# Loading w_out's diagonal blocks straight into their zeroed tile, in a causal convolution and token-mixing kernel

## The chip, the cores and the metric

The kernel runs on one core of a Trainium2 chip. The metric is the device time of one execution in microseconds; the time before the change is the median of 5 runs, 154.5 us (154.42 to 154.63).

The core has five engines that run their own instruction streams and wait for each other through semaphores. In the profile PE is TensorE (matmuls) and PEld its weight loads, DVE is VectorE, ACT is ScalarE, POOL is GpSimd and SP is SyncE. All transfers share 16 DMA engines; here GpSimd issues the loads and SyncE the stores.

## The reference

```python
def _attn_ref(x, weight):                      # x: (8, 4224, 192), weight: (8, 7)
    w = softmax(weight, axis=-1)               # 7 taps for each of 8 heads of 24 channels
    x_pad = concat([zeros((B, 6, D)), x], axis=1)
    x_unf = x_pad[:, idx, :].reshape(B, S, K, H, group)
    return einsum('hk,bskhg->bshg', w, x_unf).reshape(B, S, D)

def _moe_ref(x, w_q, w_k, w_out):              # x is the result of the convolution
    wq, wk = x @ w_q, x @ w_k                  # (B, S, 64)
    W_tok = einsum('bsd,btd->bst', wq, wk) / 8
    mixed = einsum('bst,btd->bsd', W_tok, x)   # linear attention, no softmax
    return maximum(mixed, 0) @ w_out           # (B, S, 192)
```

There is no softmax in the second part, so the kernel never forms the 4224x4224 matrix. With y the convolved input, mixed = (y w_q) (w_k' y'y) / 8: a 192x192 Gram matrix of y, a small product M = w_k' (y'y) / 8 of 64x192, and then (y w_q) M.

## The kernel before, in words

**The work.** Each of the 8 batches has 4224 tokens, kept as two halves of 2112. A batch passes these steps, by the letters that the kernel uses:

- Loads of x from DRAM, float32 to bfloat16 on the way, issued by GpSimd (`load`, `rows`, line 338, and `last`, line 355, a short last chunk), into one of NX = 5 buffers XW. Batch 0 has 8 load groups, batch 1 four, the others two.
- Y: the convolution as matmuls with a band matrix (BAND) as weights, copied out of PSUM to Y in bfloat16.
- D: a duplicate of 64 columns of Y, so that Gram blocks can be read in one run. TD: a transpose on VectorE. G: Gram matmuls into PSUM bank 7, 6 for each of 18 chunks.
- Q: 48 small matmuls, y w_q, copied out to QT by two casts on VectorE and one on ScalarE. They fill four PSUM banks.
- GEV, MC: the Gram matrix is copied out, two blocks are transposed (ident, gs), six matmuls with WK give M (gs,wk and gt,wk), which is scaled into the tile M_SB in three pieces (line 1036 on VectorE, 1035 on ScalarE).
- Z: matmuls of QT with M_SB; ReLU on the way out of PSUM to ZT (1033 on ScalarE, 1034 on VectorE). For the last 64 tokens of each half, the remainder, the tile is ZR.
- O: matmuls of ZT with w_out, copied out to one of NO = 8 slots of the ring OUT (o_sb) and stored by SyncE (line 858).

**w_out on chip.** Its rows 0 to 127 are the tile WO1. Its rows 128 to 191 are needed for both halves of the sequence at once: ZT's third part has half 0 on partitions 0 to 63 and half 1 on 64 to 127. WO2 (128 x 384) is block diagonal: the 64x192 rows stand in partitions 0 to 63, columns 0 to 191, and again in partitions 64 to 127, columns 192 to 383, and the rest is zero. One matmul against WO2 gives both halves. WO2S (128 x 192) has the same rows twice, one above the other. It is used for the remainder, and in `fused`, where Z and O matmuls of 64 partitions run side by side.

WO2S is loaded with WO1 (`wload`, lines 517 to 519, semaphore group `wl[2]`). WO2 is zeroed by GpSimd (`z_wo2`, line 534), and a job of kind W copies the two blocks from WO2S into it (lines 888 to 891).

**The order.** The string ORDER, one letter for each job, sets the order in which a planner in the kernel places jobs, and with it TensorE's order. For each copy out of PSUM the planner takes ScalarE or VectorE, whichever its cost table lets finish first; a duplicate may also go to GpSimd. CLOCK holds the planner's due times: `wq`, `wk`, `wo` say when weights are taken to be there, `fetch` how long TensorE's code is taken to be on its way. PSUM banks 0 to 6 are handed out by when they come free; a matmul waits for the copy that empties its bank. GATES ties some stores to a load: the store of block n waits until a certain group of x has landed. Block n = 5 b + i is part i of batch b; the copy into a slot of OUT waits for the store of block n - 8. SyncE issues the stores in order.

**TensorE's code.** The class Ahead cuts TensorE's instructions by branches that are never taken, with a prefetch hint each, so that its code is asked for ahead of its use, in blocks of 256 instructions.

Of the kernel before, what the change touches and what calls it, by code (L numbers as in the profile page):

```python
# [16 lines left out]


ORDER = (
    "YYYDYDYDYGTDGGGGYDYYDGTGYYDTGDGGTYTWGGGGGHQGGGTEYYMYDYWMQZZDZZZYYGGZYTGGDGAOTGOT"  # L20
    "YGZZGDOHQGTGYGGYZODOZGYGZGYYGTGGEYYGDMYGGGMTTOGHGAZGYGYYOGTYGGZGZGZQOTGTGYGGYZOG"
    "EDZZYZhGOTGHTMGGDQTMOGZZOYZGZGTZOYTGGZYGGQZGTOQGTZOYYGDZZGZGTYYOGGOEYYGGMOZDHATO"
    "GYOMGZZTGYGGTZOQGZGDOTYGZOOGAZGYGZGZTTGYGQZGOGEAZOGTTGYGMYYGGGGMODhQGZHOGAGGTYYT"
    "GGZOTGQZYGDTGYYOGOGEZZYGDGAMGYTZGGATZOYOHGZGGGTYMQGOZYZGTGYZGATGTGYGZQOOGTAZOGEY"
    "DYGGGYGGGTMAMYOOZZZGGGZDQOTZGOGAOGZTGTGAGGGQGZEOZOMZOZMOZOTZZZOOZOZOQZOZZZOOZZZO"
    "ZOOOOOO"
)


CLOCK = {  # L30
    "x0": (5.0, 7.5, 8.9, 8.1, 10.0, 11.8, 12.8, 13.6), "band": 6.5, "wq": 14.0, "wk": 16.0,
    "wo": 22.5, "fill": 24.0,
    "dma": (377e3, 13.2, 1.6, {"x": 2.2, "o": 1.2}), 
    "fetch": (64, 256, ((26.0, 8.5), (98.0, 6.4), (121.0, 7.3), (999.0, 4.8))),
}


# [192 lines left out]
def bass_lightweight_conv__then__hypermixer_token_mlp_kernel(  # L230
# [8 lines left out]
    B, S, D = x.shape  # L239
# [6 lines left out]
    wq_t, wk_t, wo_t = moe_w_q.tensor, moe_w_k.tensor, moe_w_out.tensor  # L246
# [16 lines left out]
    P = Program(nc, es)  # L263
# [50 lines left out]
    ]] + [[((0, 1), 0, 9, PAIRS), ((0, 1), 9, 18, PAIRS)]] * (B - 2)  # L314
    xg = [[P.group(f"x{b}_{g}") for g in range(len(GROUPS[b]))] for b in range(B)]
    wg = P.group("wg")
    wl = [P.group(f"wl{i}") for i in range(3)]
    og = [P.group(f"o{i}") for i in range(NO)]

    def dve(fn, deps=()):  # L320
# [2 lines left out]
    def act(fn, deps=()):  # L323
        return P.op("act", fn, deps)

    def pool(fn, deps=(), us=0.42):
        spent[0] += us
        return P.op("pool", fn, [*deps, *[o for o in P.ops["pool"] if o.dma is None][-1:]])
# [74 lines left out]
    rows(0, 1, 14, 0, 128, 3, xg[0][7], ())  # L403


    def wload(o, src, row0, width, grp, twice=1):
        spent[0] += 0.67
        n = o.shape[0]
        dims = [[width, n], [0, 2], [1, width]] if twice == 2 else [[width, n], [1, width]]
        P.dma("pool", lambda e: e.dma_start(o, bass.AP(src, row0 * width, dims)), grp)  # L410

    def warm(n, deps):
        def f(e):
# [18 lines left out]
    for j in range(5):  # L432
# [5 lines left out]
        if j == 0:  # L438
            eye = dve(lambda e: e.tensor_scalar(W_EYE[:, :], BITS[0:H, :], 127, None,
                                                op0=ALU.is_equal), [bits])  # L440
    zero = {1: [act(lambda e: e.memzero(XW[:, 1, :, NCK - 1, :]))]}
    fine = [XW[:, 0, g, 1 - g : 6 - g, :].rearrange("p c d -> p (c d)") for g in range(2)]
    x_cast = act(lambda e: e.copy(fine[0], staged[0]), [xg[0][0]])
    d = dve(lambda e: e.reciprocal(W_SM[:, :], W_SM[:, :]), [a])
# [35 lines left out]
    band = []  # L480
# [34 lines left out]
    load(1, 0)  # L515
    load(1, 1)
    wload(WO1[:, :], wo_t, 0, D, wl[2])
    wload(WO2S[0:64, :], wo_t, 128, D, wl[2])
    wload(WO2S[64:128, :], wo_t, 128, D, wl[2])
    wq = [pool(lambda e: e.tensor_copy(WQ[:, :, :], WSQ[:, :, :]), [wl[0]], 0.55)]  # L520
    z_wk = pool(lambda e: e.memset(WK[:, 3:6], 0.0))
    load(1, 2)
# [8 lines left out]
    )  # L531
    load(1, 3)
    load(2, 0)
    z_wo2 = pool(lambda e: e.memset(WO2[:, :], 0.0))
    load(2, 1)
    z_zr = pool(lambda e: e.memset(ZR[:, :, 1, :], 0.0), (), 0.34)
    for b in range(3, NX):
        load(b, 0)
# [12 lines left out]

    for o in wq:
        o.end = CLOCK["wq"]
    made = {"wq": wq, "wk": [z_wk], "wo": [z_wo2], "band": band, "ident": [ident], "z_m": [z_m], "z_zr": [z_zr]}
    done = {}

    def job_y1(b, g, k):
# [247 lines left out]
    def job_o(b, i, q):  # L805
        n = 5 * b + i
        orr = n % NO
        rem = i == 4
        tail = b == B - 1 and i == 3

        def pe(e, bk):
            kw = dict(skip_group_check=True)
            z = ZR[:, b % 2] if rem else ZT[:, (4 * b + i) % NZ]
            if rem:
                o = PS[:, bk, 0:192]
                e.matmul(o, z[:, 0, 0:128], WO1[:, :], start=True, stop=False, **kw)
                return e.matmul(o, z[:, 1, 0:128], WO2S[:, :], start=False, stop=True, **kw)
            for j in range(1 if tail else 2):
                cols = slice(q if tail else 2 * q + j, 512, 4)
                o = PS[:, bk + j, :]  # L820
                for h in range(2):
                    e.matmul(o[:, 192 * h : 192 * h + 192], z[:, h, cols], WO1[:, :],
                             start=h == 0, stop=False, **kw)
                last = e.matmul(o[:, 0:384], z[:, 2, cols], WO2[:, :], start=False, stop=True, **kw)
            return last

        def make(bk, swap=False):
            if swap:
                return [(OUT[:, orr, :, 384 * q : 384 * q + 384], PS[:, bk : bk + 2, 0:384])]
            if rem:  # L830
                return [(OUT[:, orr, 0, 0:192], PS[:, bk, 0:192])]
            if tail:
                return [(OUT[:, orr, q // 2, 384 * (q % 2) : 384 * (q % 2) + 384], PS[:, bk, 0:384])]
            return [(
                OUT[:, orr, :, 384 * q : 384 * q + 384].rearrange("p h (r d) -> p r h d", r=2),
                PS[:, bk : bk + 2, 0:384].rearrange("p r (h d) -> p r h d", h=2),
            )]

        def then():
            if not rem and q == 0 and not tail:  # L840
                return
            evs = [o for k in range(0 if not tail else q, q + 1) for o in made[("OUT", b, i, k)]]
            gate = GATES.get(n, -1)
            wait = [xg[1 + gate // 4 if gate < 4 else gate // 2][gate % (4 if gate < 4 else 2)]] * (gate >= 0)
            at = (b * S + 512 * i) * D
            if rem:
                parts = [(at + h * HALF * D, [[D, 64], [1, D]], OUT[64 * h : 64 * h + 64, orr, 0, 0:D])
                         for h in range(2)]
            elif tail:
                parts = [(at + q * D, [[4 * D, 128], [HALF * D, 2], [1, D]],  # L850
                          OUT[:, orr, q // 2, 384 * (q % 2) : 384 * (q % 2) + 384]
                          .rearrange("p (h d) -> p h d", h=2))]
            else:
                parts = [(at, [[4 * D, 128], [HALF * D, 2], [1, 4 * D]], OUT[:, orr, :, :])]
            for at, dims, src in parts:
                st = P.dma(
                    "sp",
                    lambda e, at=at, dims=dims, src=src: e.dma_start(bass.AP(out_t, at, dims), src),
                    og[orr], evs + wait,
                )  # L860
            made[("ST", n)] = [st]
            st.end = max(o.end for o in evs) + 3.0

            def landed(t, st=st):
                st.end = t

            queue["o"].append((max(o.end for o in evs) + DELAY,
                               (64 * 2 * D if rem else 128 * 2 * D if tail else 128 * 8 * D) * 4,
                               landed, GATES.get(n, -1)))
            flow()  # L870

        return Job(
            ("O", b, i, q), 1 if rem or tail else 2,
            pe, [192, 192] if rem else [192, 192, 384] * (1 if tail else 2),
            reads=[("WO", k) for k in range(2)] + [("Z", b, i, k) for k in range(1 if rem else 3)],
            evacs=[(make, ("OUT", b, i, q), 192 if rem else 384 if tail else 768, "copy")],
            then=then,
        )
# [5 lines left out]
            evacs=[(lambda bk, o=o, i=i: [(o, i)], ("WK", k), 128, "copy") for k, (o, i) in enumerate((  # L884
                (WK[0:64, 3], WK[0:64, 0]), (WK[64:128, 4], WK[64:128, 0]),
                (WK[64:128, 5], WK[64:128, 1]),
            ))]),
        Job(("W", "o", 1), 0, None, [], reads=["wo"], groups=[wl[2]],
            evacs=[(lambda bk, o=o, i=i: [(o, i)], ("WO", k), 192, "copy") for k, (o, i) in enumerate((
                (WO2[0:64, 0:D], WO2S[0:64, :]), (WO2[64:128, D : 2 * D], WO2S[64:128, :]),  # L890
            ))]),
    ]

# [75 lines left out]

    for (b, part), t in sent.items():  # L970
        put(b, part, t)
    for k, name in ((1, "wk"), (2, "wo")):
        x_at[id(wl[k])] = CLOCK[name]
    for o in band:
        o.end = CLOCK["band"]
# [180 lines left out]
    def fused(n):  # L1156
# [22 lines left out]
        def tails(e):  # L1179
            for h in range(2):  # L1180
                rows = slice(64 * h, 64 * h + 64)
                e.matmul(
                    PS[:, za[h], :], M_SB[rows, b % 2, 256 * h : 256 * h + 128],
                    QT[rows, b % 2, 512 * i : 512 * i + 512], start=True, stop=True, **kw,
                )
            for bk, z, cols in parts:
                for r in range(2):
                    for h in range(2):
                        rows = slice(64 * h, 64 * h + 64)
                        last = e.matmul(PS[:, bk + h, 192 * r : 192 * r + 192], z[rows, 2, cols[r]],  # L1190
                                        WO2S[rows, :], start=r == 0, stop=False, **kw)
            return last

        def heads(e):
# [74 lines left out]
```

## Time and profile before

| | us |
|---|---|
| median of 5 runs | 154.5 |
| lowest, highest | 154.42, 154.63 |
| profiled execution, its own time | 154.44 |
| span of its instructions | 152.6 |
| busy: PE | 137.3 (90%) |
| busy: ACT | 128.4 (84%) |
| busy: DVE | 119.5 (78%) |
| busy: POOL | 59.5 (39%) |

The TensorE clock granted in the profiled execution was 0.99 of full speed. 40.84 MB were moved, 268 GB/s over the span. The 16 DMA engines are busy for nine tenths or more of nearly every slice of the span up to 115 us. The loads (queue q0) took 73.9% of the engines' time, the stores and the few loads of SyncE (q1) 48.9%; the shares overlap. The packets of TensorE's code are a queue of their own, 19 packets of 0.31 MB in all.

How to read the rows that follow: a row of the chain gives start, length and what ran; a row of a timeline gives start, length, engine, line, operation, output<-input with shapes, and in brackets how long the engine stood idle before it and what ended that. A row of DMA issues ends with size and microseconds from issue to landing. Line numbers are those of the kernel before.

### The profile page before, as it was taken

How to read it: one execution, taken by the hardware profiler on the slowest of the kernel's cores; microseconds unless marked ns; L12 is line 12 of the kernel's file. 1: busy time of each engine (PE TensorE's matmuls, PEld its weight loads, DVE VectorE, ACT ScalarE, POOL GpSimd, SP SyncE). 2: the span in 40 equal slices, each digit the busy share in tenths (PEclk: the TensorE clock that was granted, in tenths of full speed). 3: DMA queues.
4: the chain of work that ended last, by engine and by line, in shares of the span. 5: the costliest groups of instructions: out<-in, count | busy, mean ns of one | idle time of the engine just before them, and what ended most of it. 6: DMA issues, size and time to landing. Idle time of an engine off the chain costs nothing.

```text
span 152.6 us, 5675 instructions
## 1 busy us (share of the span) xinstructions
PE 137.3 (90%) x2432; PEld 100.9 (66%) x2457; DVE 119.5 (78%) x241; ACT 128.4 (84%) x212; POOL 59.5 (39%) x77
## 2 busy tenths in 40 slices
PE   5977787999999999999999999999899999999920
PEld 1366565777767777677776777678577778766710
DVE  5674889966997877888988859999998977795710
ACT  5556598999998899988999989899898888999930
POOL 7999999989755801635200022030110300000000
PEclk9999999999999999999999999999999999999996
DMA  3999999999999999999999999999999978499896
GB/s 95 260 202 181 190 190 176 194 189 194 190 193 193 222 345 335 282 191 293 340 340 212 196 343 338 306 187 314 410 391 404 385 278 337 172 391 379 304 359 202
DMA packets 48984, 40.84 MB, mean 268 GB/s; under 512 B 37312, under 2 KB 41024, under 8 KB 48960
## 3 DMA queue, kind: packets, MB, share of 16 engines
q0 software_dynamic: 36384, 13.35, 73.9%
q1 hardware_dynamic: 12576, 27.14, 48.9%
q8 instruction: 19, 0.31, 0.7%
q14 instruction: 5, 0.04, 0.1%
HBM read 27.86 MB, written 25.95 MB: 353 GB/s over the span
## 4 chain that ended last, share of the span: by engine, by line
PE 74%; POOL 13%; DVE 5%; issue 3%; ACT 0%; ACTq 0%; POOLq 0%
PE ps L207 74%; POOL xw L338 7%; POOL wk L410 1%; DVE m_sb L1036 1%; DVE zt L1034 1%; POOL xw L355 1%; DVE zr L1034 1%; POOL wo2s L410 1%; DVE wo L1030 1%; DVE yb L1026 1%; DVE o_sb L1030 1%; DVE qt L1030 1%; POOL m_sb L523 1%; POOL wo L410 0%; POOL wq L520 0%
## 5 line engine op out<-in xcount | busy, mean ns | idle before, releaser
L1030 ACT COPY o_sb<-ps 128x768 f32<-128x768 f32 (+2 forms) x62 | 47.0, 772 | 3.5 <-PE ps L207 2.3
L207 PE MATMUL ps<-wo,zt 128*128 128x192 bf16 (+1 forms) x358 | 47.6, 271 | 0.8 <-DVE o_sb L1030 0.2
L1030 ACT CAST y<-ps 128x864 bf16<-128x864 f32 (+6 forms) x50 | 40.5, 838 | 5.4 <-PE ps L207 4.9
L207 PEld LDWEIGHTS ps<-y 128*128 128x128 bf16 (+1 forms) x864 | 35.5, 98 | 12.3 <-issue 2.4
L207 PE MATMUL ps<-y 128*128 128x64 bf16 (+1 forms) x864 | 40.2, 193 | 1.7 <-DVE yb L1026 0.6
L207 PEld LDWEIGHTS ps<-wo,zt 128*128 128x128 bf16 x358 | 31.9, 115 | 9.1 <-DVE o_sb L1030 0.6
L1030 POOL COPY y<-y 128x1152 bf16<-128x1152 bf16 x12 | 13.8, 1148 | 57.5 <-ACT y L1030 34.5
L1026 DVE STREAM_TRANSPOSE yb<-y 128x576 int32<-128x576 int32 x48 | 35.7, 759 | 0.1
L1034 DVE TENSOR_SCALAR zt<-ps 128x512 bf16<-128x512 f32 x46 | 30.7, 681 | 5.5 <-PE ps L207 5.2
L207 PE MATMUL ps<-xw,band 128*128 128x432 bf16 (+5 forms) x192 | 32.1, 286 | 2.6 <-DMA xw<-in_x_dram 1.2
L338 POOL DMA_DIRECT2D xw<-in_x_dram x35 | 32.1, 927 | 2.0 <-POOL xw L497 1.1
L1033 ACT ACTIVATE zt<-ps 128x512 bf16<-128x512 f32 x50 | 29.2, 604 | 1.7 <-PE ps L207 1.6
L207 PE MATMUL ps<-qt,m_sb 128*128 128x512 bf16 (+2 forms) x95 | 22.0, 334 | 1.4 <-DVE m_sb L1036 1.0
L1030 DVE CAST y<-ps 128x864 bf16<-128x864 f32 (+2 forms) x18 | 18.4, 1024 | 4.6 <-PE ps L207 4.1
L207 PEld LDWEIGHTS ps<-xw,band 128*128 128x128 bf16 x192 | 13.3, 97 | 8.3 <-DMA xw<-in_x_dram 1.6
L1030 DVE CAST qt<-ps 128x288 bf16<-128x288 f32 (+1 forms) x32 | 12.2, 424 | 7.7 <-PE ps L207 7.6
L207 PE MATMUL ps<-yb,wq 32*64 32x288 bf16 x768 | 15.3, 284 | 0.6 <-DVE y L1030 0.3
L1030 ACT CAST qt<-ps 128x576 bf16<-128x576 f32 x16 | 10.3, 643 | 4.3 <-PE ps L207 3.6
L207 PEld LDWEIGHTS ps<-qt,m_sb 128*128 128x128 bf16 (+1 forms) x120 | 8.9, 96 | 5.4 <-DVE m_sb L1036 1.1
L207 PEld LDWEIGHTS ps<-yb,wq 32*64 32x64 bf16 x768 | 10.6, 102 | 2.6 <-issue 0.7
L1030 DVE COPY o_sb<-ps 128x192 f32<-128x192 f32 (+2 forms) x12 | 7.4, 613 | 1.3 <-PE ps L207 1.0
L207 PE MATMUL ps<-warm 128*128 128x256 bf16 (+1 forms) x22 | 6.8, 434 | 1.3 <-DVE warm L389 1.3
(65 smaller groups left out, 73.1 us busy)
## 6 DMA issues: line engine op xcount, KB each, us to landing
out_dram<-o_sb SPq DMA_DIRECT2D x31, 768.0 KB, 7.4
xw<-in_x_dram POOLq DMA_DIRECT2D x14, 432.0 KB, 15.8
xw<-in_x_dram POOLq DMA_DIRECT2D x14, 384.0 KB, 16.9
o_sb<-in_x_dram SPq DMA_DIRECT2D x2, 480.0 KB, 4.7
out_dram<-o_sb SPq DMA_DIRECT2D x16, 48.0 KB, 6.0
out_dram<-o_sb SPq DMA_DIRECT2D x4, 192.0 KB, 2.4
xw<-in_x_dram POOLq DMA_DIRECT2D x2, 240.0 KB, 6.5
xw<-in_x_dram POOLq DMA_DIRECT2D x1, 288.0 KB, 6.9
```

The lines of the kernel that those rows point to most:

```text
L207: return self.e.matmul(*a, **k)
L338: return e.dma_start(XW[lo:hi, b % NX, half, c : c + n, :], bass.AP(x_t, at, [[D, hi - lo], [CW * D, n], [1, D]]),)
L355: lambda e: e.dma_start(XW[0:hi, b % NX, :, NCK - 1, :], bass.AP(x_t, at, [[D, hi], [HALF * D, 2], [1, D]]),),
L410: P.dma("pool", lambda e: e.dma_start(o, bass.AP(src, row0 * width, dims)), grp)
L523: z_m = pool(lambda e: e.memset(M_SB[:, :, :], 0.0), (), 0.85)
L1026: return e.transpose(o, i)
L1030: return e.copy(o, i) if eng == "act" else e.tensor_copy(o, i)
L1033: return e.activation(o, i, AF.Relu)
L1034: return e.tensor_scalar(o, i, 0.0, None, op0=ALU.max)
L1036: else e.tensor_scalar(o, i, scale, None, op0=ALU.mult))
```

## The change

WO2 is zeroed on ScalarE, early, instead of on GpSimd. The two blocks of w_out are loaded straight into WO2, in the place where WO2S was loaded, and these loads wait for the zeroing. The W job with the two copies is gone, and so is its letter in ORDER. WO2S is loaded by two later DMAs, behind the loads of batch 2, under a semaphore group of its own, `wl[3]`, for which the remainder's O matmuls wait. `fused` reads its 64-partition operands from the blocks of WO2. O jobs wait for the group `wl[2]` itself. Three due times in CLOCK are changed. With the new due times the planner also gives a few copies to other engines: near 20 to 27 us two casts of Y go from ScalarE to VectorE, one piece of M_SB and one ReLU from VectorE to ScalarE, and one duplicate of batch 2 goes from GpSimd to VectorE. Apart from that the order on each engine stays as it was.

```diff
-    "YYYDYDYDYGTDGGGGYDYYDGTGYYDTGDGGTYTWGGGGGHQGGGTEYYMYDYWMQZZDZZZYYGGZYTGGDGAOTGOT"
+    "YYYDYDYDYGTDGGGGYDYYDGTGYYDTGDGGTYTWGGGGGHQGGGTEYYMYDYMQZZDZZZYYGGZYTGGDGAOTGOTY"
...
-    "wo": 22.5, "fill": 24.0,
+    "wo": 21.0, "wo2": 36.0, "fill": 24.0,
...
-    "fetch": (64, 256, ((26.0, 8.5), (98.0, 6.4), (121.0, 7.3), (999.0, 4.8))),
+    "fetch": (64, 256, ((26.0, 6.6), (98.0, 6.1), (121.0, 6.5), (999.0, 4.8))),
...
-    wl = [P.group(f"wl{i}") for i in range(3)]
+    wl = [P.group(f"wl{i}") for i in range(4)]
...
-    def wload(o, src, row0, width, grp, twice=1):
+    def wload(o, src, row0, width, grp, twice=1, deps=()):
...
+    z_wo2 = act(lambda e: e.memzero(WO2[:, :]))
     fine = [XW[:, 0, g, 1 - g : 6 - g, :].rearrange("p c d -> p (c d)") for g in range(2)]
...
     wload(WO1[:, :], wo_t, 0, D, wl[2])
-    wload(WO2S[0:64, :], wo_t, 128, D, wl[2])
-    wload(WO2S[64:128, :], wo_t, 128, D, wl[2])
+    wload(WO2[0:64, 0:D], wo_t, 128, D, wl[2], 1, [z_wo2])
+    wload(WO2[64:128, D : 2 * D], wo_t, 128, D, wl[2], 1, [z_wo2])
...
     load(2, 0)
-    z_wo2 = pool(lambda e: e.memset(WO2[:, :], 0.0))
     load(2, 1)
+    for h in range(2):
+        wload(WO2S[64 * h : 64 * h + 64, :], wo_t, 128, D, wl[3])
...
-            reads=[("WO", k) for k in range(2)] + [("Z", b, i, k) for k in range(1 if rem else 3)],
+            reads=[("Z", b, i, k) for k in range(1 if rem else 3)],
+            groups=[wl[2], wl[3]] if rem else [wl[2]],
...
-        Job(("W", "o", 1), 0, None, [], reads=["wo"], groups=[wl[2]],
-            evacs=[(lambda bk, o=o, i=i: [(o, i)], ("WO", k), 192, "copy") for k, (o, i) in enumerate((
-                (WO2[0:64, 0:D], WO2S[0:64, :]), (WO2[64:128, D : 2 * D], WO2S[64:128, :]),
-            ))]),
...
-                                        WO2S[rows, :], start=r == 0, stop=False, **kw)
+                                        WO2[rows, D * h : D * h + D], start=r == 0, stop=False, **kw)
```

More of the change, by code (lines that the diff above doesn't have):

```diff
@@ L19 @@
 ORDER = (
-    "YYYDYDYDYGTDGGGGYDYYDGTGYYDTGDGGTYTWGGGGGHQGGGTEYYMYDYWMQZZDZZZYYGGZYTGGDGAOTGOT"
[L21 to L26, printed above, removed]
+    "YYYDYDYDYGTDGGGGYDYYDGTGYYDTGDGGTYTWGGGGGHQGGGTEYYMYDYMQZZDZZZYYGGZYTGGDGAOTGOTY"
+    "GZZGDOHQGTGYGGYZODOZGYGZGYYGTGGEYYGDMYGGGMTTOGHGAZGYGYYOGTYGGZGZGZQOTGTGYGGYZOGE"
+    "DZZYZhGOTGHTMGGDQTMOGZZOYZGZGTZOYTGGZYGGQZGTOQGTZOYYGDZZGZGTYYOGGOEYYGGMOZDHATOG"
+    "YOMGZZTGYGGTZOQGZGDOTYGZOOGAZGYGZGZTTGYGQZGOGEAZOGTTGYGMYYGGGGMODhQGZHOGAGGTYYTG"
+    "GZOTGQZYGDTGYYOGOGEZZYGDGAMGYTZGGATZOYOHGZGGGTYMQGOZYZGTGYZGATGTGYGZQOOGTAZOGEYD"
+    "YGGGYGGGTMAMYOOZZZGGGZDQOTZGOGAOGZTGTGAGGGQGZEOZOMZOZMOZOTZZZOOZOZOQZOZZZOOZZZOZ"
+    "OOOOOO"
 )
@@ L409, in wload @@
         dims = [[width, n], [0, 2], [1, width]] if twice == 2 else [[width, n], [1, width]]
-        P.dma("pool", lambda e: e.dma_start(o, bass.AP(src, row0 * width, dims)), grp)
+        P.dma("pool", lambda e: e.dma_start(o, bass.AP(src, row0 * width, dims)), grp, deps)
     def warm(n, deps):
@@ L553, in bass_lightweight_conv__then__hypermixer_token_mlp_kernel @@
         o.end = CLOCK["wq"]
-    made = {"wq": wq, "wk": [z_wk], "wo": [z_wo2], "band": band, "ident": [ident], "z_m": [z_m], "z_zr": [z_zr]}
+    made = {"wq": wq, "wk": [z_wk], "band": band, "ident": [ident], "z_m": [z_m], "z_zr": [z_zr]}
     done = {}
@@ L971, in bass_lightweight_conv__then__hypermixer_token_mlp_kernel @@
         put(b, part, t)
-    for k, name in ((1, "wk"), (2, "wo")):
+    for k, name in ((1, "wk"), (2, "wo"), (3, "wo2")):
         x_at[id(wl[k])] = CLOCK[name]
```

## The prediction

> **What bounds the kernel now.** I read the chain of work that ended last first, then the timelines of the engines around the change, then the transfers, because this kernel fills TensorE, ScalarE and the DMA queues at once. The chain, in order of time, columns start, length, what:
>
> ```profile
> 19.64 1.99 POOL xw L338 x2
> 21.63 0.48 POOL wo L534
> 22.11 0.02 issue
> 22.14 0.80 DVE wo L1030
> 22.93 0.03 issue
> 22.96 0.21 DVE wo L1030
> 23.17 0.03 issue
> 23.21 0.36 DVE m_sb L1036
> 23.57 0.27 issue
> 23.84 3.36 PE ps L207 x47
> ```
>
> Up to 23.8 us the end is set by GpSimd issuing loads; the last links are the memset of WO2 (L534), the two copies into it, and the scaling into M_SB that stands behind them on VectorE. From 23.84 us on the chain is TensorE almost alone. So what the stage before 24 us gives back can reach the end, unless something later was only just in time. The timeline of TensorE and VectorE there (start, length, engine, line, what, idle before):
>
> ```profile
> 21.23 0.25 PE L207 MATMUL ps<-gt,wk 128*128 128x64 bf16 x3
> 21.81 1.01 PE L207 MATMUL ps<-yb,wq 32*64 32x288 bf16 x48 [0.32 <-DVE y L1030]
> 22.14 1.04 DVE L1030 COPY wo<-wo2s 64x192 bf16<-64x192 bf16 x2 [0.35 <-POOL wo L534]
> 22.47 0.38 ACT L1035 ACTIVATE m_sb<-ps 64x128 bf16<-64x128 f32 x2
> 22.88 0.64 ACT L1030 CAST qt<-ps 128x576 bf16<-128x576 f32 x1
> 23.48 0.75 DVE L1030 CAST qt<-ps 128x288 bf16<-128x288 f32 x2
> 23.84 1.05 PE L207 MATMUL ps<-qt,m_sb 128*128 128x512 bf16 x4 [1.02 <-DVE m_sb L1036]
> 24.04 1.58 ACT L1033 ACTIVATE zt<-ps 128x512 bf16<-128x512 f32 x3 [0.52 <-PE ps L207]
> 24.28 0.11 PEld L207 LDWEIGHTS ps<-qt,m_sb 128*128 128x128 bf16 x2 [0.34 <-DVE qt L1030]
> ```
>
> TensorE stands 1.02 us for M_SB, and the fourth of its Z matmuls waits for the VectorE casts of QT, which stand behind the same copies. In the busy rows by stage TensorE then has 54.77 us of 55.70 (24 to 79.7 us) and 50.25 of 51.80 (89.2 to 141 us). What else could be late next is a transfer. The timeline of ScalarE at 79 us, and the store that was issued at 67.13 us (size, us to landing):
>
> ```profile
> 79.27 0.60 ACT L1033 ACTIVATE zt<-ps 128x512 bf16<-128x512 f32 x1
> 79.77 0.79 ACT L1030 COPY o_sb<-ps 128x768 f32<-128x768 f32 x1
> 80.48 0.88 ACT L1030 CAST y<-ps 128x864 bf16<-128x864 f32 x1
> ```
>
> ```profile
> out_dram<-o_sb SPq DMA_DIRECT2D x1, 768.0 KB, 12.3
> ```
>
> The OUT ring has 8 slots. The copy at 79.77 us is the first into slot 7 for block 15 (batch 3, i = 0) and must wait for the store of block 7, landed at 67.13 + 12.3 = 79.44 us. Its slack is 0.33 us, the smallest of all 32 reuses (the next are 1.37, 1.41 and 1.78 us, for blocks 20, 18 and 14).
>
> **The change, part by part.** Times are of the profiled run: 154.44 us, span 152.6, so 1.84 us lie around the span; the median of the runs is 154.5, 0.06 above.
>
> 1. *The copies leave VectorE.* Gone are 0.35 us of waiting for L534 and 1.04 us of copies. The built order also moves work: VectorE takes two of ScalarE's casts of Y (864 elements: 1.06 us on VectorE, 0.89 on ScalarE), ScalarE takes the 64x192 scaling (0.32; it was 0.35 on VectorE) and one 128x512 relu (0.60; 0.69). ScalarE gets 1.78 - 0.92 = 0.86 us lighter by 28 us, VectorE 2.12 - 1.04 - 0.35 - 0.69 = 0.04 heavier. New times: ScalarE's first Y cast of the pair at 20.76 ends near 21.6, the three M_SB pieces (0.32 + 0.38) by 22.3; their matmuls ended at 21.48. So M_SB is no longer last: the Q matmuls end at 22.82, and Z can start at 22.9 instead of 23.84, 0.93 earlier. What is late next are the evacuations. VectorE ends its duplicate at 21.79, then the new Y cast at 22.85, then the QT casts by 23.6 instead of 24.23: 0.6 earlier for the fourth Z. ScalarE ends its QT cast at 23.52 and starts the first relu there instead of at 24.04: 0.5 earlier. I take a lead of 0.60; bounds 0.5 and 0.93. A loss is excluded in this stage, since neither engine gets 0.1 us more work than before.
> 2. *Zeroing WO2 on ScalarE.* One more memset like L441 (0.345 us) between L441, which starts at 2.6 us, and the cast L443, before which ScalarE idles 2.0 us for a DMA: 0. The GpSimd loads of WO2 wait for it at 12.7 us, nine microseconds after it is done: 0, also for the WQ cast and batch 1's loads queued behind them.
> 3. *GpSimd's queue.* The memset (0.48) goes, two issues of WO2S (1.18, the row of L410 at 12.67) come behind batch 2. The loads of batches 3 and 4 are issued 0.70 later. Their time to landing rises from 6.4 us for a load issued at 18 us to 13.3 us at 28 us, so they wait in the DMA queue, not for the issue: 0. Were the queue empty: 0.70 on these loads, of which TensorE sees nothing, as batch 3's first part landed at 39.74 and was first read at 42.38, 2.6 us of slack.
> 4. *New waits of TensorE.* For the w_out loads at 27.2 us (landed by 20.2) and for WO2S at the first remainder, 43.7 us. WO2S lands right behind batch 2 (its last load: 23.79 + 10.2 = 34.0), at about 34.3, nine microseconds early. Both 0.
> 5. *A duplicate of batch 2 moves from GpSimd (1.16 us at 35.36) to VectorE.* The 576-element copies there took 0.28 to 0.61, so twice that is 0.6 to 1.2 us; it goes ahead of a relu before which VectorE idled 0.83. I take 0, at most 0.4, and that on an engine which has 16.55 us busy of 20.
> 6. *More bytes in the load queue.* 128 rows of 768 bytes. Batch 1's third part landed at 15.71 + 6.7 = 22.4, its fourth, 1,024 rows, at 18.00 + 6.4 = 24.4: 2.0 ns a row, so 0.26 us. Upper bound: the three w_out loads before the third part. The second part landed at 19.5, so w_out and the 1,112 rows of the third part took 2.9 us together, 0.7 of it w_out. Lower bound 0. Every later load, and the stores that are gated on loads, shift by 0.26: block 7's store lands at 79.70.
>
>    The Trainium skill speaks against this step: its page "DMA: Bandwidth & Descriptors", section Bandwidth (Measured), says that transfers under 64 KB are descriptor-dominated and gives 0.68 us for 4 KB and 0.95 for 64 KB. By an estimate from that page two 24 KB loads would cost about 1.6 us of queue, block 15 would be 1.3 us later than now, and the sum would end near 155. The rows above price three such loads at 0.7, so I go by them.
> 7. *The lead meets the ring.* With a lead of 0.60 ScalarE wants slot 7 at 79.17; it may have it at about 79.75. Its lead is gone there (79.77 before). TensorE keeps more: the Q matmuls at 81.87 need the banks that the cast at 80.48 empties, at 81.36, so TensorE can hold 81.87 - 81.42 = 0.45. ScalarE gains again where it had idled for TensorE: 0.21 at 82.89, then 0.18 at 88.55 and 0.33 at 89.21. By 90 us both have some 0.4. Bounds: 0.02 (ScalarE's lead at the ring sets all) and 0.60 (nothing lost). I take 0.40, as the idle rows exist.
> 8. *To the end.* The other ring slacks (1.37 and more, less 0.26) exceed the lead. The last full stores are issued when their copies end (141.15 for a copy that ended at 141.12), so the lead carries over one to one.
>
> Sum: 154.44 - 0.60 + 0.20 = 154.04; on the median 154.1.
>
> **The rivals.**
> A. *The ring takes nothing*: the lead stays 0.6 to 0.9, 153.6 to 153.9. For it: TensorE runs ahead by several banks, and ScalarE is 0.86 us lighter. Against: ScalarE waits in order, 0.33 us is less than 0.60.
> B. *The ring takes all*: 154.4 to 154.5. For it: ScalarE is busy 8.79 of 9.5 us after the ring. Against: the three idle rows.
> C. *Slower: TensorE's code comes late.* Its code is fetched in blocks through the same DMA engines. From a prefetch hint to the end of the block's packet took 5.0 to 10.1 us; counted in instructions, with blocks of 256 as the class Ahead has them and the hinted one 380 after its hint, the blocks hinted at 50.85 and 57.57 us came only 0.28 and 0.25 us before TensorE reached them, 8.65 and 8.62 us after the hint. With TensorE 0.6 us earlier against the loads and stores, another latency is drawn. It decides if one of these two exceeds 8.9; at 10.1 TensorE stands 1.2 us. Less the lead that is 0.6 of loss, and no more to lose at the ring: 155.0. Against: before, none of the hints stalled TensorE.
> D. *Slower through the ring*: two loads dearer than 1.0 us shift slot 7 past what TensorE can hold. Against: 0.7 is the upper bound by rows; 154.8 at 1.1.
>
> **How the numbers follow.** About 0.2%, 0.31 us, is what a measurement of this kernel can tell from no change: faster means below 154.19. Forecast (154.0 to 154.3) 0.40, A 0.27, B 0.15, C 0.13, D 0.05. Four fifths of the forecast's share, with A, are faster: 0.59, taken as 0.60; B and the rest of the forecast are the same: 0.23, taken as 0.22; C and D slower: 0.18. The likeliest case gives 154.1. The range reaches down through most of A, 153.6, and up to part of C and D, 154.8. The forecast's own range is 153.95 to 154.35.
>
> **What would show it.** Step 1: the Z matmuls start near 22.9 us, no wait of TensorE for M_SB, the fourth Z by 23.7. Step 6: the loads of batch 3 land 0.2 to 0.4 later, block 7's store at 79.6 to 79.9. Step 7: ScalarE's copy of block 15 shows idle time before it, released by a DMA; TensorE's lead is 0.6 before 79 us and about 0.4 after 90. Rival A shows no such idle time. C shows TensorE idle for "issue" over 0.3 us after a branch hint. The prediction is wrong if the lead at 28 us isn't near 0.6, or if the copy of block 15 doesn't wait.

## The result, and the profile after

The changed kernel takes 154.14 us in the median of 25 executions, the kernel before 154.54 in the median of the 46 beside it: a ratio of 0.9965, interval 0.9952 to 0.9978. The ratios, here and below, are of means, from which two slow executions of experiments are left out (157.09 and 156.67 us) while a few of the kernel before near 156 us are kept, so they lie up to 0.2% below the ratios of the medians, which is 0.9974 here. By the medians the change gains 0.40 us, a quarter of a per cent; 154.1 was forecast. But the executions do not sit at their median. Ten of the 25 took 153.65 to 153.86 us, eight 153.95 to 154.34, six 154.37 to 154.51 and one 155.03. The profiled execution is one of the early ones: 153.70 us, span 151.9.

Its chain of waits around the change (start, length, what; line numbers differ from those of the kernel before by one or two, and again in the experiments):

```profile
20.18 1.58 DVE y L1029 x2
21.77 0.02 issue
21.79 1.02 PE ps L207 x47
22.81 0.02 issue
22.83 0.78 DVE qt L1029 x2
23.61 0.14 issue
23.74 2.27 PE ps L207 x27
```

GpSimd, the memset and the two copies are gone from it. What is left is Y, the Q matmuls, VectorE's two casts of QT, and Z. The timeline there:

```profile
21.51 0.74 ACT L1034 ACTIVATE m_sb<-ps 64x192 bf16<-64x192 f32 x3
21.68 1.03 DVE L1029 CAST y<-ps 128x864 bf16<-128x864 f32 x1
21.79 0.99 PE L207 MATMUL ps<-yb,wq 32*64 32x288 bf16 x48 [0.32 <-DVE y L1029]
22.70 0.33 PEld L207 LDWEIGHTS ps<-qt,m_sb 128*128 128x128 bf16 x3 [0.23 <-issue]
22.93 0.59 PE L207 MATMUL ps<-qt,m_sb 128*128 128x512 bf16 x2 [0.16 <-DVE y L1029]
23.37 1.58 ACT L1032 ACTIVATE zt<-ps 128x512 bf16<-128x512 f32 x3
23.71 0.13 PEld L207 LDWEIGHTS ps<-qt,m_sb 128*128 128x128 bf16 x2 [0.68 <-ACT qt L1029]
23.74 0.59 PE L207 MATMUL ps<-qt,m_sb 128*128 128x512 bf16 x2 [0.22 <-DVE qt L1029]
```

The weight loads of Z in the profile of before:

```profile
23.61 0.33 PEld L207 LDWEIGHTS ps<-qt,m_sb 128*128 128x128 bf16 x3 [1.09 <-DVE m_sb L1036]
```

M_SB is now complete at 22.25 (21.51 + 0.74), before the Q matmuls end at 22.78. Both profiles have five weight loads of Z and only four matmuls: the record of the first matmul is missing. By the weight loads Z starts at 22.70 instead of 23.61, and its fourth matmul is loaded at 23.71 instead of 24.28 (the row is in the prediction). The 0.16 us before 22.93 is the missing record and no wait: in three later executions of the same program the first Z matmul is recorded at 22.69 to 22.72, with no idle time before it. For the same reason the wait for M_SB before was nearer 0.8 us (22.82 to 23.61) than 1.02. What is left is 0.22 us for the casts of QT. Now ScalarE at the ring, and the store of block 7 (size, us to landing):

```profile
78.47 0.60 ACT L1032 ACTIVATE zt<-ps 128x512 bf16<-128x512 f32 x1
78.96 0.79 ACT L1029 COPY o_sb<-ps 128x768 f32<-128x768 f32 x1
79.67 0.88 ACT L1029 CAST y<-ps 128x864 bf16<-128x864 f32 x1
```

```profile
out_dram<-o_sb SPq DMA_DIRECT2D x1, 768.0 KB, 11.5
```

Block 15's copy starts 0.81 us earlier than before and waits for nothing, because the store, issued at 66.86, landed at 78.40, a microsecond earlier than in the profile of before. In this execution hardly any of the lead was lost: ScalarE's copies near the end lie 0.76 us ahead (140.94 for 141.70), and the time is 0.74 lower.

Called lead below is how much earlier TensorE starts the first Y matmul of a load group than in the kernel before, where it starts at 24.73 (batch 1, third part), 57.64 (batch 4) and 92.38 us (batch 6). Here it is 0.56, 0.80 and 0.80.

### The profile page after: what moved, and what is told of

It reads as the page before. It is cut to its first block, busy times and chain, and to the rows that moved or that the text cites. A ratio compares the mean times of both kernels' runs of the same rounds, so it can differ in the third digit from the quotient of the medians.

```text
span 151.9 us, 5674 instructions
## 1 busy us (share of the span) xinstructions
PE 136.5 (90%) x2432; PEld 100.9 (66%) x2457; DVE 120.8 (80%) x240; ACT 127.8 (84%) x213; POOL 59.1 (39%) x77
## 4 chain that ended last, share of the span: by engine, by line
PE 76%; DVE 8%; DMA 5%; issue 3%; POOL 3%; ACT 0%; ACTq 0%; POOLq 0%
PE ps L207 76%; DMA xw<-in_x_dram 5%; POOL xw L338 2%; DVE y L1029 2%; DVE yb L1025 2%; DVE qt L1029 1%; DVE zt L1033 1%; DVE zr L1033 1%; DVE m_sb L1035 1%; DVE o_sb L1029 1%; ACT o_sb L1029 0%; ACTq L155 0%; POOL bits L397 0%; POOLq L397 0%; POOLq L1253 0%
## 5 line engine op out<-in xcount | busy, mean ns | idle before, releaser
L207 PE MATMUL ps<-wo,zt 128*128 128x192 bf16 (+2 forms) x410 | 51.0, 267 | 0.8 <-DVE o_sb L1029 0.2
L1029 ACT CAST y<-ps 128x864 bf16<-128x864 f32 (+6 forms) x48 | 39.0, 834 | 5.4 <-PE ps L207 4.9
L207 PEld LDWEIGHTS ps<-wo,zt 128*128 128x128 bf16 (+1 forms) x410 | 35.0, 114 | 10.4 <-ACT zt L1032 0.7
L1029 POOL COPY y<-y 128x1152 bf16<-128x1152 bf16 x11 | 12.6, 1144 | 57.1 <-ACT y L1029 34.5
L1033 DVE TENSOR_SCALAR zt<-ps 128x512 bf16<-128x512 f32 x45 | 30.0, 680 | 4.6 <-PE ps L207 4.3
L1032 ACT ACTIVATE zt<-ps 128x512 bf16<-128x512 f32 x51 | 29.8, 604 | 1.3 <-PE ps L207 1.1
L1029 DVE CAST y<-ps 128x864 bf16<-128x864 f32 (+2 forms) x20 | 20.5, 1026 | 4.7 <-PE ps L207 4.2
L1029 DVE CAST qt<-ps 128x288 bf16<-128x288 f32 (+1 forms) x32 | 12.3, 424 | 7.6 <-PE ps L207 7.4
L207 PE MATMUL ps<-warm 128*128 128x256 bf16 (+1 forms) x22 | 6.0, 394 | 1.3 <-DVE warm L389 1.3
```

The lines of the kernel that those rows point to most:

```text
L207: return self.e.matmul(*a, **k)
L1029: return e.copy(o, i) if eng == "act" else e.tensor_copy(o, i)
L1032: return e.activation(o, i, AF.Relu)
L1033: return e.tensor_scalar(o, i, 0.0, None, op0=ALU.max)
```

## The experiments

The theory at the outset: the stage before 24 us gives a lead, and the ring of OUT takes back what it does not fit. The rivals: the ring takes nothing; the lead is another size or comes from the moved casts; the added load harms by itself. Each run has the kernel before beside it, at 154.53 to 154.55 us in the median. The last three have one execution of it, of 156.2 us, which is not used; their leads are taken against the profile of before, like all others.

**Nine slots, changed kernel.**

```diff
-    NO = 8
+    NO = 9
```

> The changed kernel with a ninth slot in the OUT ring, all else and all engine assignments the same. The changed kernel's executions lie between 153.65 and 155.0 us, 11 of 25 at or under 153.8 and the others from 153.9 up. Theory R (the ring): the later executions are those in which a store lands after ScalarE wants its slot (the slacks were 0.56, 0.64 and 0.71 us in the profiled one). A ninth slot moves each reuse some 4 us later, so all executions come to 153.6 to 153.8 and the spread goes. Rival C (TensorE's code comes late in some executions): the ring does not matter, median near 154.1 and the same spread. Rival P (the load landings before 50 us stall TensorE directly): as C.

Measured: 153.60 us (152.95 to 154.00, 9 executions), ratio 0.9924, interval 0.9898 to 0.9951. The cluster above 154 is gone. The spread was expected to go too, and did not: it is still a microsecond wide, with two executions at 152.95 and 153.10. (The expectation's 11 of 25 at or under 153.8 are nine by the list of times.) In the profiled execution the store of block 7 came late, at 79.95:

```profile
79.00 0.79 ACT L1029 COPY o_sb<-ps 128x768 f32<-128x768 f32 x1
79.71 0.88 ACT L1029 CAST y<-ps 128x864 bf16<-128x864 f32 x1
```

```profile
out_dram<-o_sb SPq DMA_DIRECT2D x1, 768.0 KB, 12.7
```

Block 15 no longer uses block 7's slot, and its copy starts 0.95 us before that store is down. With eight slots it would have waited. In its new slot, which block 6 used before it, the copy has 2.91 us of slack. This kernel beats the kernel before and, narrowly, by the two intervals, the changed kernel with eight slots.

**Nine slots, kernel before.** The same edit there.

> The kernel before with a ninth slot in the OUT ring. Theory R: the kernel before does not wait at the ring, its smallest slack being 0.33 us: 154.4 to 154.6, ratio 0.999 to 1.001. If the ring was holding the kernel before in most executions, it gets faster by 0.2 us or more and the change would have gained less than it seems.

Measured: 154.44 us (154.27 to 156.01, 12), ratio 0.9989, interval 0.9961 to 1.0018: no difference. This is as expected: the ring did not hold the kernel before, although here too the store of block 7 was as late as 79.83, with the copy at 79.76. So what nine slots give the changed kernel is the lead that the change made.

**Without the loads of WO2S.** The remainder's O matmul reads WO2's first block columns instead.

```diff
-    WO2S = sbuf("wo2s", [128, D], BF16)
...
-    for h in range(2):
-        wload(WO2S[64 * h : 64 * h + 64, :], wo_t, 128, D, wl[3])
...
-                return e.matmul(o, z[:, 1, 0:128], WO2S[:, :], start=False, stop=True, **kw)
+                return e.matmul(o, z[:, 1, 0:128], WO2[:, 0:D], start=False, stop=True, **kw)
...
-            groups=[wl[2], wl[3]] if rem else [wl[2]],
+            groups=[wl[2]],
...
```

> The changed kernel without the two late loads of WO2S; the remainder's second matmul reads the first 192 columns of WO2 instead, so half of the remainder's tokens come out without their share of w_out's last 64 rows; all other work is the same. Step 6 of the prediction puts the two loads at 0.26 us of the load queue. With theory R the loads and the gated stores come 0.26 us earlier, the ring slacks grow by that, and fewer executions are late: median 153.75 to 154.0. If the loads cost the queue nothing, or rival C holds: median near 154.1, spread as in the changed kernel.

Measured: 153.84 us (153.72 to 154.53, 12), ratio 0.9952, interval 0.9928 to 0.9977. Eight executions took 153.72 to 153.88; four took 154.20 to 154.53. So the late executions are there without the added rows, which are not their cause, though they may make them more frequent: 4 of 12 here and 13 of 25 in the changed kernel are above 154.1, too few to tell.

**The wait alone.** In the kernel before, WO2 is zeroed on ScalarE, the copies stay.

```diff
+    z_wo2 = act(lambda e: e.memzero(WO2[:, :]))
...
-    z_wo2 = pool(lambda e: e.memset(WO2[:, :], 0.0))
```

> The kernel before with one part of the change alone: WO2 zeroed early on ScalarE, no longer by GpSimd at 21.6 us. The two copies on VectorE, the loads and all assignments stay. By step 1 VectorE's wait of 0.35 us goes and M_SB is ready 0.35 us earlier, so the Z matmuls start near 23.5 instead of 23.84: a lead of 0.35, 154.1 to 154.3 where it is kept. If the wait was worth nothing because the casts of QT set the fourth Z matmul anyway: they stand behind the same copies, so they too come 0.35 earlier. Rival: the lead is lost later (ring slack 0.33): 154.4 to 154.5.

Measured: 154.09 us (153.84 to 155.00, 12), ratio 0.9962, interval 0.9937 to 0.9987. The timeline:

```profile
21.93 0.84 DVE L1030 COPY wo<-wo2s 64x192 bf16<-64x192 bf16 x2
22.81 0.35 DVE L1036 TENSOR_SCALAR m_sb<-ps 64x192 bf16<-64x192 f32 x1
23.08 0.75 DVE L1030 CAST qt<-ps 128x288 bf16<-128x288 f32 x2
23.44 1.05 PE L207 MATMUL ps<-qt,m_sb 128*128 128x512 bf16 x4 [0.65 <-DVE m_sb L1036]
```

Z starts 0.40 earlier, where 0.35 was expected, and not by the wait alone. The copies start only 0.21 earlier, at 21.93 instead of 22.14, since the duplicate ahead of them takes 0.84 us here and 0.60 before; and they take 0.84 instead of 1.04. Why these lengths change the runs do not tell. The lead of 0.40 stays the same to batches 4 and 6, and the time of the profiled execution is 0.38 lower. So moving the memset alone gives half of the changed kernel's lead; in the median it is worth as much as the whole change.

**More load in the queue.** Five blocks of 128 rows, used by nothing, behind WO2S.

```diff
+    PAD = sbuf("pad", [128, 5, D], BF16)
...
+    P.dma("pool", lambda e: e.dma_start(PAD[:, :, :], bass.AP(x_t, 0, [[D, 128], [CW * D, 5], [1, D]])), wl[3])
```

> The changed kernel with 640 more rows of 768 bytes in the load queue, one DMA of x into a spare tile right behind WO2S, landing counted in the same group as WO2S. At 2.0 ns a row every later load and gated store comes 1.3 us later, five times step 6; assignments the same. Ring theory: block 7's store lands at 79.7 to 81.2 instead of 78.4 to 79.9, ScalarE wants its slot at 79.0, so it waits 0.7 to 2.2 us; by step 7 TensorE holds back up to 0.45 of each loss: 154.3 to 155.6, every execution above 154.1, and the profile shows idle time of ScalarE before the copy at 79 us, released by a DMA. If loads have 2 us of slack everywhere and the ring is not the cause: 153.7 to 154.5 as without it.

Measured: 155.52 us (154.75 to 157.09, 12), ratio 1.0053, interval 1.0020 to 1.0086. The chain of waits around 80 us:

```profile
68.80 12.22 DMA out_dram<-o_sb
81.02 0.02 issue
81.04 0.02 ACTq L166
81.05 0.04 issue
81.09 0.80 ACT o_sb L1031
81.89 0.79 ACT y L1031
```

The chain leaves TensorE, and the store of block 7 holds ScalarE for 1.85 us. What the change gained, and more, is lost there: TensorE's lead is 0.63 us at batch 4 and -0.96 at batch 6.

**The same with nine slots.**

> The same 640 rows more, with nine slots in the OUT ring. Smallest reuse slack with nine slots was 2.9 us, so 1.3 us fit: ring theory 153.5 to 153.9, like nine slots without the extra rows (153.6). If the extra rows hurt through anything else (late loads of x, late code): as slow as the run with eight slots, 154.3 to 155.6.

Measured: 153.55 us (153.19 to 154.23, 8), ratio 0.9917, interval 0.9881 to 0.9953. The store lands at 81.11, the copy of block 15 starts at 79.22, and TensorE's lead is 0.55 at batch 4 and 0.54 at batch 6. So the large loss comes through that slot. A small one is left that comes ahead of it: in the two profiles with more rows batch 3's first part lands at 41.40 and 41.48 us (38.58 to 39.95 in those of the changed kernel), its first Y matmul starts at 41.75 and 41.83 instead of 41.58, and by batch 4 the lead is 0.63 and 0.55 instead of 0.80. In the median of nine slots this does not show (153.55 against 153.60), but the expectation's 153.5 to 153.9 holds only five of the eight.

**The old due times.** The `fetch` row of CLOCK as before. The planner then leaves the Y casts on ScalarE and the duplicate on GpSimd, and gives all pieces of M_SB to VectorE. Besides the zeroing, the copies and the loads only this differs from the kernel before, which had two of the pieces on ScalarE.

```diff
-    "fetch": (64, 256, ((26.0, 6.6), (98.0, 6.1), (121.0, 6.5), (999.0, 4.8))),
+    "fetch": (64, 256, ((26.0, 8.5), (98.0, 6.4), (121.0, 7.3), (999.0, 4.8))),
```

> The changed kernel with the kernel before's due times for TensorE's code. The planner then leaves the duplicate of batch 2 on GpSimd and both Y casts on ScalarE and gives all three M_SB pieces to VectorE; WO2's loads stay as in the change. VectorE: duplicate to 21.8, three pieces (0.35, 0.30, 0.22) to 22.6, QT casts behind Q's end at 22.8, so the Z matmuls still start near 22.95 and the fourth near 23.7. ScalarE is 0.86 us heavier by 28 us. Theory: the lead comes from the copies that are gone, 0.5 to 0.6 at 30 us; the moved casts add the 0.2 that takes it to 0.75 to 0.8. Fastest executions 153.85 to 153.95, median 154.0 to 154.2. Rival: the moved casts are most of the gain: lead 0.3 or less, 154.3 to 154.5.

Measured: 153.91 us (153.82 to 156.67, 12), ratio 0.9951, interval 0.9921 to 0.9980. The lead is 0.65 at 24 us, 0.68 at batch 4 and 0.67 at batch 6, so the theory's 0.5 to 0.6 was a little low, and the rival's 0.3 is out. Of the changed kernel's 0.80, by differences between the runs, some 0.1 comes from the moved copies, 0.40 from moving the memset and the rest, 0.28, from dropping the copies into WO2. The median is below the 154.0 to 154.2 expected, and below the changed kernel's: four of its twelve executions are above 154.1, 13 of 25 there, too few to say that the moved copies cost anything.

**The changed kernel again, one execution.**

> The changed kernel once more, for a second look at its ring. In an execution at 153.9 us or more, ScalarE stands before the copy at 79 us, or at one near 91.7 or 97.7 (blocks 18 and 20), for a DMA; in one at 153.8 or less it stands at none.

Measured: 154.44 us. The chain of waits and the timeline of ScalarE:

```profile
67.70 12.31 DMA out_dram<-o_sb
80.01 0.02 issue
80.03 0.02 ACTq L166
80.05 0.04 issue
80.09 0.80 ACT o_sb L1029
80.89 0.79 ACT y L1029
81.68 0.14 issue
81.81 0.95 PE ps L207 x44
```

```profile
78.45 0.60 ACT L1032 ACTIVATE zt<-ps 128x512 bf16<-128x512 f32 x1
80.09 0.80 ACT L1029 COPY o_sb<-ps 128x768 f32<-128x768 f32 x1 [1.04 <-PE ps L207]
```

The same program, and now ScalarE stands 1.04 us at block 15. The bracket names PE, but the chain names the store that landed at 80.01, 0.08 us before the copy. The lead is 0.81 at batch 4 and 0.05 at batch 6.

**Three more executions of it**, to see whether the time follows that landing, with a rule fixed beforehand.

> One more profiled execution of the changed kernel, unaltered, to see whether its time follows ScalarE's wait for block 7's store at block 15. Theory (ring decides each execution): ScalarE wants slot 7 at 78.96; the wait w is the landing of block 7's store plus 0.08 us less 78.96; the time is 153.7 for w = 0 (store landed before 78.9) and 153.7 + w - 0.3 where w is over 0.3, since a wait of 1.04 cost 0.74 in the look before. Rival (the spread comes from elsewhere, from TensorE's code, or from the clock): a time over 154.0 with w under 0.2, or one under 153.9 with w over 0.6.

> The same kernel once more, with the same two rules: the theory has 153.65 to 153.9 where block 7's store lands before 79.1 us, and 153.7 + (landing + 0.08 - 78.96) - 0.3 where it lands later, to within 0.15; the rival has a time that does not follow that landing.

> The same kernel a third time, same rules. By the 25 timed executions, of which 10 were at 153.9 or less, the theory expects about one or two of these three looks with no wait at block 15 and the others with a wait of 0.3 to 1.3 us; the rival expects no wait at block 15 in looks that took over 154.0.

Measured: 153.72, 153.67 and 154.30 us. For the landings of the table below the rule has 153.65 to 153.9 for the first two and 154.40 to within 0.15 for the third, and all three fit. ScalarE in the third of them, and the chain that leads to it:

```profile
78.49 0.60 ACT L1033 ACTIVATE zt<-ps 128x512 bf16<-128x512 f32 x1
79.96 0.80 ACT L1030 COPY o_sb<-ps 128x768 f32<-128x768 f32 x1 [0.87 <-DMA out_dram<-o_sb]
```

```profile
67.37 12.51 DMA out_dram<-o_sb
79.88 0.02 issue
79.90 0.02 ACTq L167
79.92 0.04 issue
79.96 0.80 ACT o_sb L1030
80.76 0.79 ACT y L1030
81.55 0.14 issue
81.68 8.34 PE ps L208 x183
```

All five profiled executions of the changed kernel together, in us:

| store of block 7: issued | landed | block 15's copy starts | lead at batch 4 | lead at batch 6 | time |
|---|---|---|---|---|---|
| 66.86 | 78.40 | 78.96 | 0.80 | 0.80 | 153.70 |
| 66.83 | 78.41 | 78.97 | 0.79 | 0.79 | 153.72 |
| 66.97 | 78.45 | 78.95 | 0.82 | 0.81 | 153.67 |
| 67.37 | 79.88 | 79.96 | 0.79 | 0.18 | 154.30 |
| 67.70 | 80.01 | 80.09 | 0.81 | 0.05 | 154.44 |

Up to batch 4 they are alike to 0.03 us. Where the store lands in time, the lead goes through to the end; where it lands late, the copy is shifted by 1.00 and 1.13 us and TensorE loses 0.61 and 0.76, which is 0.39 and 0.37 less than the shift. In the run with the added rows the shift is about 1.95 (81.09 against 79.14, which is the 79.22 of its nine-slot partner less the 0.08 by which TensorE was ahead of that one), the loss 1.59, so 0.36 less. Three late executions give the same room of TensorE, 0.36 to 0.39 us. The clock does not go with the time: granted were 0.994 of full speed in the execution of 154.30 us and 0.987 in that of 153.70.

## Why the prediction was right

**The number** was right: 154.1 forecast, 154.14 measured, inside the range and on the likely side. It was right as the middle of a spread, for which the prediction had one value, and in that there is luck: only eight of the 25 executions took the forecast's own 153.95 to 154.35, and the median falls there because ten are earlier and seven later. Two errors also cancelled, as step 7 shows. By the prediction's own signs of being wrong, a lead at 28 us that isn't near 0.6 or a copy of block 15 that doesn't wait, it was not wholly right: the lead at 28 us is 0.75, and in three of the five profiled executions that copy does not wait. Its working, by its steps:

1. *The copies leave VectorE.* Shown right in mechanism and at 23 us to 0.05: Z without a wait for M_SB, and the fourth Z at 23.74 (23.7). The 23.84 of before and the 22.93 now are the second Z matmul, as said above; by the weight loads Z starts 0.91 earlier, where 0.93 was forecast. The term was mis-sized: 0.60 taken, 0.56 at the first Y of batch 1's third part, but 0.75 at `fused`, 0.80 by batch 3. The bounds of 0.5 and 0.93 hold it. What was missed is a second gain after the fourth Z: with the old due times the lead is 0.65 and then 0.68, with the new ones 0.56 and then 0.80. That it comes from ScalarE, which the moved copies make lighter, fits these numbers but was not tested by itself. Nor did the 0.35 us of waiting go as such: the run with the memset alone shows 0.21 from an earlier start and 0.20 from shorter copies.
2. *Zeroing on ScalarE*: 0, shown. It took 0.35 us at 2.84, and the three loads of w_out were issued by 13.85 us, as before.
3. *GpSimd's queue*: 0, as forecast. The first loads of batch 3 are issued 0.63 later (0.70 forecast), and their landing does not follow: 38.6 to 40.0 us in five executions, before it was 39.74. So the sign named for step 6, a landing 0.2 to 0.4 later, is not seen either.
4. *New waits*: 0. WO2S landed at 34.01 to 35.34 (34.3 forecast), seven to nine microseconds before its use.
5. *The duplicate*: 0.60 us on VectorE, and the idle time before the next ReLU fell from 0.83 to 0.16. Nothing lost, as forecast.
6. *More bytes*: the price was near, its consequence was not. WO2S is complete 0.34 to 0.40 us after batch 2's last part in the five executions (0.26 taken, 0 to 0.7 the bounds), and the 768 rows with the dummy load took 1.59 us, 2.1 ns a row, where 2.0 was read from the profile of before. The step failed where it added 0.26 to one landing, 79.44, as if that were fixed: block 7's store landed at 78.40 to 80.01 in the same program. Only one of the five, at 79.88, lies in the 79.6 to 79.9 that was forecast.

   The Trainium skill's page "DMA: Bandwidth & Descriptors", section Bandwidth, under Measured, has transfers under 64 KB as descriptor-dominated, and the estimate from it was 1.6 us for these two loads, with the sum near 155. In this full queue they cost 0.34 to 0.40 us; the measurement decides, and the page's figures do not fit these loads, which stand in a queue behind others.
7. *The lead meets the ring.* Shown right, in place, direction and mechanism, for the executions that are late: the copy of block 15 waits for block 7's store, and nothing else takes the lead. The room is near too: the step has TensorE hold 0.45, its terms (a slip of 0.58 for ScalarE, 0.20 lost by TensorE) leave 0.38, and the late executions show 0.36 to 0.39. Where TensorE stands is only in part as forecast: in the executions of 154.44 and 154.30 us it stands 0.37 and 0.20 us before Y matmuls at 80.94 and 80.81, until the copy of block 15 itself has emptied their banks, and 0.16 before the Q matmuls. What failed is the one landing and the one want: 79.70 against 79.17. Measured are wants at 78.96 and landings on both sides of it, so there are executions without any wait, and in those that wait the copy starts 0.08 after the landing whatever the lead was. By the measured want and room, a landing at 79.70 gives a shift of 0.82, a loss of 0.44 and 154.14 us. The errors of steps 1 and 7 cancelled: where the store is late, a larger lead only waits longer.
8. *To the end* one to one: shown to within 0.06. A lead of 0.80 at batch 6 is 0.74 in the time, 0.18 is 0.14, 0.05 is 0.00.

**The rivals.** A (the ring takes nothing, 153.6 to 153.9) is what three of five profiled and ten of 25 timed executions did. B (it takes all, 154.4 to 154.5) is the execution at 154.44. The forecast, A and B are one mechanism at three landing times and should have been written so. C did not come: the row of TensorE's waits for "issue" is the same before, after and in the execution of 154.44 us:

```profile
PE ps L207 <- issue: 0.6, 4, 0.2
```

D (slower through the ring by dear loads) was shown to exist, with five times the rows, and not at the change's own size.

That the kernel before is steadier fits this, though its room was not measured. Its copy starts at 79.77, so with the same room a landing up to 79.69 + 0.38 = 80.07 costs it nothing; the changed kernel is safe only to 78.88 + 0.38 = 79.26.

## What to carry to other kernels

A lead gained early ends at the first buffer whose release does not move with it; look up that release and its slack before pricing the lead, and then look at how far the release wanders from execution to execution, since one profile shows one draw. If the wander is larger than the slack, the result is a spread and not a number, and the cure is one more buffer: here a ninth slot turned a ratio of 0.9965 into 0.9924, and a median of 154.14 into 153.60. And try the cheapest part alone: moving one memset gave half of the lead, and as good a median as the whole change.

## What the runs showed that was not expected

The same program's transfers are not repeatable to a microsecond, though TensorE up to batch 4 is, to 0.03 us. Over the five executions batch 2's first part landed at 29.27 to 30.96 us and batch 4's first at 47.55 to 49.28; block 7's store was issued at 66.83 to 67.70, as SyncE's queue of stores waits there for batch 5's first part (65.83 to 66.70), and took 11.5 us in the three early executions and 12.3 and 12.5 in the two late ones. Batch 2's first part comes before the added loads in the queue, so the wandering does not begin with them. Where it does, the runs do not tell, nor why the landing of 768 KB takes 11.5 us in some executions and 12.3 or more in others.

A bracket that names TensorE as what ended an idle time can hide a store: at 80.09 us it did, and the chain of waits named the right one.

With nine slots some executions fell to 152.95 and 153.10, and with the added rows to 153.19 and 153.22, below anything that the leads here account for: a lead of 0.80 from 154.44 gives 153.64. Their cause stays open.
